# Threshold attention and a squared-ReLU layer: own buffers for the low words' integers, and own step orders for the first two periods

## The chip, the cores and the metric

The kernel runs on one core of a Trainium2 chip. Its engines work side by side and meet through semaphores: PE (TensorE, matrix products and transposes; PEld is its weight load), DVE (VectorE), ACT (ScalarE), POOL (GpSimd) and SP (SyncE, which here only issues DMAs). The metric is the device time of one execution in microseconds (us); the median of three runs is given.

## The reference

Attention over 8 batches, 8 heads, 576 rows and head size 64, in which only scores within `tau` of their row's maximum count; its output, rearranged to 4608 rows of 512, goes through two matrix products with a squared ReLU between them. `q`, `k`, `v` are float32; `w_in` and `w_out` come as float64.

```python
scores = scale * np.matmul(q, k.transpose(0, 1, 3, 2))
thresh = np.max(scores, axis=-1, keepdims=True) - tau
scores = np.where(scores >= thresh, scores, -1000000000.0)
scores = scores - np.max(scores, axis=-1, keepdims=True)
attn = np.exp(scores)
attn = attn / (np.sum(attn, axis=-1, keepdims=True) + 1e-09)
attn_out = np.matmul(attn, v).astype(np.float32)
...
x = np.ascontiguousarray(attn_out.transpose(0, 2, 1, 3)).reshape(B * S, H * D)
h = np.maximum(x @ w_in, 0.0)
return (h * h @ w_out).astype(np.float32)
```

## The kernel before, in words

The kernel has three stages: attention (up to about 510 us of the profile), the first matrix product (`hidden_layer`, line 825) and the second (`output_layer`, line 960). The two products are done by a scheme with fewer multiplications, which needs sums and differences of blocks of the operands; much of POOL's and DVE's work is that. The change touches the attention stage only.

**Units and periods.** The 64 heads are taken as 32 pairs (two heads side by side in 128 partitions). A pair's 576 rows make four units of 128 rows; the last 64 rows of two pairs share a fifth unit. A period (`period(p)`, line 608) starts two units, A = 2p and B = 2p + 1, and finishes the two before. Within a period the order on every engine is the order in which a list of step names is gone through; there are two lists, `PLAIN` (line 592) and `CONVERTING` (line 597), the second for periods in which a weight chunk is converted (p = 2 to 34). Each engine executes its own instructions strictly in that order. The steps that matter here:

- `SA`, `SB` (`scores`, line 423; PE at L434): the scores of A and B, into a PSUM tile `sc` of six banks. A0 means unit A, first head; B1 unit B, second head.
- `topA0` ... `topB1` (L452, DVE): the row minimum of the negated scores, with a copy of the scores to SBUF.
- `powA0` ... `powB1` (L462, ACT): the exponentials. `leastA`, `leastB` (L459, POOL): the threshold.
- `maskA0` ... `maskB1` (L467, DVE): the exponentials are set to zero below the threshold, and summed. It has two inputs in SBUF.
- `over`, `inv` (L474 POOL, L477 DVE): the reciprocal of the sums.
- `U`, `V`, `W` (`fill`; PE at L380 and L515) with `eU`, `eV`, `eW` (`filled`; ACT at L523): the weights are transposed through PSUM; `U` and `V` use the one buffer of the pool `pt`, `W` the middle banks of `sc`.
- `PV` (L532, PE): weights times `v`. `x`, `xm` (L642, L654): its eviction, its scaling, and the store of x to DRAM (L578).
- `T` (`turn_some` and `turn`, PE at L398) with `eT` (ACT at L403 and L411): q or k of a later pair is transposed, into what `spots()` gives (banks 1 and 4 of `sc`, which also hold scores), and evicted. q of pair 1 is turned in period 0, k of pair 1 in period 1, q of pair 2 in period 2. When `eT` is gone through, it also asks for the loads of a later pair (`ask_ahead`, line 343): after pair 0 that is pair 1, after pair 1 both pairs 2 and 3.
- `fetch` (line 178; SP at L191): the load of a weight chunk, 128 x 1024 words of 32 bits, for the period after the next.
- `c1` to `c6` (`convert1` to `convert6`): a float64 chunk becomes float32 with integer operations on its low and high words, which lie alternately in the buffer `raw`. `c1` (L205, ACT) takes the high words' absolute value, `c2` (L212, POOL) scales the low words to integers in place, `c3` (L219, POOL) clamps, `c4` and `c5` (L227, L235, DVE) shift and merge, `c6` (L245, POOL) adds the two. A chunk's `c1`, `c2` and `c3` stand in one period, `c4` to `c6` in the next: chunk 0 begins in period 2, chunk 1 in period 3.

**Queues.** Nearly all DMAs are issued by SP, in the order of the steps; each takes SP some 0.4 to 0.6 us. There are eight semaphores for them in turn, so a DMA is issued only when the eighth before it has landed. Loading q of a pair takes two DMAs (L294), loading k seven (L308 four times, L315 twice, L316 once). A load of v is one (L326).

**Banks.** Each PSUM access is declared by `touch` (line 355): two accesses to the same bank by different engines wait for each other, others do not. So a `top` that reads bank 1 waits for a turn that was written to bank 1 ahead of it in the list.

**Start.** Lines 1014 to 1031: loads of pair 0, some transposes of the identity that write nothing of use (`keep_busy`), the turns of pair 0, then the periods from p = -2; after period 0 come 20 more such transposes.

The arena is one SBUF tile that is cut up by hand (`Region`, line 19); `cv` is the region of the conversion's buffers.

Of the kernel before, what the change touches and what calls it, by code (L numbers as in the profile page):

```python
# [10 lines left out]
FP32 = mybir.dt.float32  # L11
# [37 lines left out]
def kernel(  # L49
# [49 lines left out]
    ARENA = 27264  # L99
    X_SIZE = 7 * BANK + 3 * 7 * P  # L100
    X_AT = (ARENA - X_SIZE, ARENA - 2 * X_SIZE)
    arena = ctx.enter_context(tc.tile_pool(name="arena", bufs=1)).tile([P, ARENA], FP32, name="arena")
    sb, cv = Region(arena, 0, X_AT[0]), Region(arena, X_AT[0], ARENA)

    ident = const.tile([P, P], FP32, name="ident")
    make_identity(nc, ident)
# [101 lines left out]

    def convert2(m):
        if m in parts:  # L210
            lo = parts[m][0]
            nc.gpsimd.tensor_scalar(out=lo, in0=lo.bitcast(U32), scalar1=2.0**-29, scalar2=None, op0=ALU.mult)  # L212

    def convert3(m):
        if m not in parts:
# [175 lines left out]
    def turn(i, which, spots, other=None):  # L391

        nat, to = loaded.pop((i, which)), places(i)
        of = [nat[:, t, :] for t in range(FULL)] + ([loaded.pop((i, 2))] if which else [])
        for t, x in enumerate(of):
            for r, (spot, at) in enumerate(spots):
                rows = ds(r * HALF, HALF)
                made = nc.tensor.transpose(spot[:, ts(t, HALF)], x[rows, :], ident[rows, rows])  # L398
                touch("turns", made, at, BANK)
        half = FULL * HALF  # L400

        def scaled(to, spot):
            touch("turned", nc.scalar.activation(out=to, in_=spot[0], func=AF.Identity, scale=qscale[:, :]), spot[1], BANK, i)  # L403

        def then():
            part = lambda r, x, n: (spots[r][0][:, ds(x, n)], spots[r][1])
            if which:
                for r, n in ((0, half), (1, half + REST)):
                    spot = part(r, 0, n)
                    copy_by = other if r and other else nc.scalar.copy  # L410
                    touch("turned", copy_by(to[1][:, ds(r * half, n)], spot[0]), spot[1], BANK, i)  # L411
                scaled(to[2], part(0, half, REST))
                ask_ahead(i, 1)
            else:
                for r in range(2):
                    scaled(to[0][:, ds(r * half, half)], part(r, 0, half))
                ask_ahead(i, 0)

        return then
# [179 lines left out]
        powA1 powB0 c4 eT inv x maskA1 maskA0 W leastB maskB0 c5 eV c2 powB1 c6 eW maskB1 xm  # L599
    """.split()  # L600

    def spots():
        return [(sc[:, ds(b * BANK + REST, (FULL + 1) * HALF)], b * BANK) for b in (1, 4)]

# [3 lines left out]
    def period(p):  # L608

        A, B_, a, b = 2 * p, 2 * p + 1, 2 * p - 2, 2 * p - 1  # L610
        m, turns = p - 2, TURNS.get(p, ())
        late, pt = {"W": []}, {}

        def fills(f, m):
            if has(2 * m):
                pt[f] = pt_pool.tile([P, 2, BANK], FP32, tag="pt", name="pt")
                fill(m, f, pt[f])

        def evict(f, m):
            if has(2 * m):  # L620
                filled(m, f, pt[f], 2 * BANK if f == "W" else None)

        def W():
            if has(2 * m + 2):
                pt["W"] = middle()
                fill(m + 1, "W", pt["W"], 2 * BANK)

        def turn_some():
            late["turn"] = [turn(g // 2, g % 2, spots()) for g in turns]

        def PV():
            if has(2 * m):
                values(m)

        def values_out():
            if not has(2 * m):
                return
            late["x"] = x = sb.tile([P, 2, P], FP32, tag="x", bufs=2, name="x")
            for j in range(2):
                from_ = sc[:, ds(5 * j * BANK, P)]  # L640
                if converts(p):
                    made = nc.scalar.copy(x[:, j, :], from_)  # L642
                else:
                    made = nc.vector.tensor_tensor(  # L644
                        out=x[:, j, :], in0=from_, in1=wT[m][:, ts(SCALE_AT + j, P)], op=ALU.mult
                    )
                touch("x", made, 5 * j * BANK, P, m)

        def given_out():
            if has(2 * m):  # L650
                x = late.pop("x")
                if converts(p):
                    both = x[:, :, :].rearrange("p j n -> p (j n)")
                    nc.gpsimd.tensor_tensor(out=both, in0=both, in1=wT[m][:, ds(SCALE_AT * P, 2 * P)], op=ALU.mult)  # L654
                wT.pop(m)
                valued(m)
                give_x(m, x)
            ask(False)

        def scored_a():  # L660
            if has(A):
                scores(A, False)
                scores(A, True)
                scores(B_, True)
                softmax(A)

        def scored_b():
            if has(A):
                scores(B_, False)
                softmax(B_)  # L670

        def every(key):
            for then in late.get(key, ()):
                then()

        steps = {
            "U": lambda: fills("U", m), "V": lambda: fills("V", m + 1), "W": W, "T": turn_some,
            "eU": lambda: evict("U", m), "eV": lambda: evict("V", m + 1), "eW": lambda: evict("W", m + 1),
            "eT": lambda: every("turn"),
            "SA": scored_a, "SB": scored_b,  # L680
            "PV": PV, "x": values_out, "xm": given_out,
            "c1": lambda: convert1(begun(p)), "c2": lambda: convert2(begun(p)),
            "c3": lambda: convert3(begun(p)), "c4": lambda: convert4(begun(p - 1)),
            "c5": lambda: convert5(begun(p - 1)), "c6": lambda: convert6(begun(p - 1)),
            "s1": lambda: sums_due(p) and sums_step(), "s2": lambda: sums_due(p) and p < 60 and sums_step(), "fetch": lambda: fetch(begun(p + 2)),
        }
        steps["over"] = lambda: do(a, "over")
        steps["inv"] = lambda: do(a, "inverse")
        for letter, n in (("A", A), ("B", B_)):
            for what, name in (("least", "least"),):  # L690
                steps[what + letter] = lambda n=n, name=name: do(n, name)
            for what, name in (("top", "top"), ("pow", "power"), ("mask", "mask")):
                for j in range(2):
                    steps[f"{what}{letter}{j}"] = lambda n=n, name=name, j=j: do(n, name, j)
        for name in CONVERTING if converts(p) else PLAIN:
            steps[name]()
        for n in (A, B_):
            if has(n) and units[n][1] == FULL:
                for i in units[n][0]:
                    turned.pop(i)  # L700
# [301 lines left out]
    with tc.manual_schedule():  # L1002
        with ExitStack() as stack:
            sc = stack.enter_context(tc.tile_pool(name="sc", bufs=1, space=PSUM)).tile([P, 6 * BANK], FP32, name="sc")
            pt_pool = stack.enter_context(tc.tile_pool(name="pt", bufs=1, space=PSUM))

            def keep_busy(times, to=None):

                if to is None:
                    to = pt_pool.tile([P, 2, BANK], FP32, tag="pt", name="idle")[:, 0, 0:P]  # L1010
                for _ in range(times):
                    nc.tensor.transpose(to, ident[:, :], ident[:, :])

            load_q(0)
            load_k(0)
            read_tau()
            first = sb.tile([P, 4, 4], FP32, tag="small", bufs=4, name="small")
            nc.scalar.activation(out=first[:, 0, :], in_=ident[:, 0:4], func=AF.Exp)
            load_v(0)
            keep_busy(15)  # L1020
            pq = pt_pool.tile([P, 2, BANK], FP32, tag="pt", name="pq")
            turn(0, 0, [(pq[:, r, :], None) for r in range(2)])()
            keep_busy(8, sc[:, ds(5 * BANK, P)])
            turn(0, 1, spots(), nc.vector.tensor_copy)()
            for i in range(1, 3):
                load_v(i)
            for p in range(-2, NU // 2 + 3):
                period(p)
                if p == 0:
                    keep_busy(20)  # L1030
                if X_FIRST <= p < X_FIRST + 4:
                    load_x(0, XPARTS[p - X_FIRST :][:1])
                if p == X_FIRST + 4:
                    summing.append(prepare_x(0, lambda op, out, x, y: op(nc.gpsimd, out, x, y)))
            for _ in range(60):
                sums_step()
            ask()
# [186 lines left out]
```

## Time and profile before

| | us |
|---|---|
| median of 3 runs | 1307.08 (1306.43 to 1308.34) |
| the profiled execution's own time | 1308.12 |
| its span, first to last instruction | 1306.3 |
| attention stage | 0 to about 510 |
| first product (PE L825) | about 512 to 880 |
| second product (PE L960) | about 924 to 1306 |

The page's first part gives each engine's busy share of the span: PE 98%, DVE 77%, ACT 65%, POOL 70%. These are averages over three stages with different limits. The second part shows DVE at nine tenths or more in 14 of the first 15 of 40 slices of 32.7 us, that is in most of the attention stage, and PE at nine tenths from its second slice on. The groups of the conversion on POOL are L212 (32 times, 2035 ns each), L245 (32 times, 1479 or 1478 ns) and L219 (32 times, 613 ns). Start and length of single instructions are read from the timeline, whose rows are: start, length, engine, line, operation, what it writes and reads, how many were merged, and in brackets the idle time before it with what ended that.

### The profile page before, as it was taken

What the parts mean: (1) busy time and instruction counts of PE and PEld (TensorE: products, weight loads), DVE (VectorE), ACT (ScalarE), POOL (GpSimd) and SP (SyncE); (2) the same over time, 40 slices, a digit from 0 to 9 for tenths busy, and PEclk for the clock granted to TensorE, in tenths of its full rate; (3) what the DMA queues carried; (4) which work ended last, traced back from release to release, by engine and by line L of the source; (5) the groups of instructions that cost most, each with busy time, mean ns of one, the idle gap of its engine ahead of it and who ended that gap; (6) DMA issues with size and microseconds to landing.
All of it is one profiled execution on the core that took longest, in us unless ns stands there. A gap on an engine that the chain in (4) does not pass through costs nothing.

```text
span 1306.3 us, 47872 instructions
## 1 busy us (share of the span) xinstructions
PE 1284.5 (98%) x19483; PEld 1159.8 (89%) x19483; DVE 1010.8 (77%) x2431; ACT 845.7 (65%) x1498; POOL 916.4 (70%) x1023
## 2 busy tenths in 40 slices
PE   8999999999999999999999999999999999999998
PEld 5777777677777777999999999999999999999998
DVE  5999999999999996877787778777646654665463
ACT  5999999888898985657665766675523432433240
POOL 2777778755555320978897789768777777777775
PEclk9999999999999999999999999999999999999999
DMA  6565666544333313466556665569645234522511
GB/s 153 145 160 140 169 182 188 147 103 104 89 78 79 79 41 80 133 200 218 182 181 194 203 208 164 180 247 393 245 158 162 63 105 158 162 68 96 162 34 33
DMA packets 247035, 192.12 MB, mean 147 GB/s; under 512 B 97184, under 2 KB 195488, under 8 KB 246816
## 3 DMA queue, kind: packets, MB, share of 16 engines
q1 hardware_dynamic: 245504, 188.66, 48.5%
q8 instruction: 153, 2.51, 0.8%
q14 instruction: 66, 0.54, 0.2%
q10 hardware_dynamic: 1312, 0.41, 0.1%
HBM read 116.65 MB, written 72.35 MB: 145 GB/s over the span
## 4 chain that ended last, share of the span: by engine, by line
PE 87%; ACT 5%; DMA 3%; DVE 3%; issue 1%; POOL 1%; SPq 0%; ACTq 0%; DVEq 0%; POOLq 0%
PE po L960 29%; PE ph L825 28%; PE sc L532 11%; PE sc L434 10%; PE pt L380 5%; DVE arena L452 3%; ACT arena L462 2%; PE sc L515 2%; DMA wall<-w 2%; PE sc L398 2%; ACT arena L523 1%; PE sc L380 1%; DMA g<-arena 1%; ACT arena L403 0%; ACT c L771 0%
## 5 line engine op out<-in xcount | busy, mean ns | idle before, releaser
L125 POOL TENSOR_TENSOR arena<-arena 128x512 f32<-128x512 f32 (+1 forms) x314 | 378.1, 1223 | 129.1 <-DVE arena L125 115.1
L960 PE MATMUL po<-wall,arena 128*128 128x128 f32 x3528 | 394.7, 275 | 1.4 <-ACT arena L737 1.4
L960 PEld LDWEIGHTS po<-wall,arena 128*128 128x128 f32 x3528 | 394.3, 192 | 1.8 <-ACT arena L737 1.8
L825 PE MATMUL ph<-arena,wall 128*128 128x128 f32 x3528 | 394.2, 275 | 0.7 <-DVE arena L644 0.7
L825 PEld LDWEIGHTS ph<-arena,wall 128*128 128x128 f32 x3528 | 394.0, 192 | 0.8 <-issue 0.8
L125 DVE TENSOR_TENSOR arena<-ph,arena 128x512 f32<-128x512 f32 x378 | 256.3, 688 | 86.3 <-PE ph L825 63.2
L122 POOL TENSOR_TENSOR arena<-arena 128x128 f32<-128x128 f32 (+2 forms) x314 | 255.4, 814 | 53.8 <-DMA arena<-w 37.6
L125 DVE TENSOR_TENSOR arena<-po,arena 128x128 f32<-128x128 f32 x378 | 108.4, 290 | 168.6 <-PE po L960 164.5
L467 DVE SCALAR_TENSOR_TENSOR arena<-arena 128x576 f32<-128x576 f32 x288 | 237.4, 860 | 1.3 <-POOL arena L459 0.8
L452 DVE TENSOR_SCALAR_CACHE_REDUCE arena<-sc 128x576 f32<-128x576 f32 x288 | 205.0, 747 | 14.6 <-ACT arena L523 4.8
L462 ACT ACTIVATE arena<-arena 128x576 f32<-128x576 f32 x288 | 208.1, 773 | 11.8 <-DVE arena L452 8.5
L771 ACT COPY c<-arena 128x512 f32<-128x512 f32 (+1 forms) x303 | 173.5, 579 | 49.6 <-DVE arena L122 41.7
L532 PEld LDWEIGHTS sc<-arena 64*64 64x64 f32 x5760 | 159.2, 133 | 36.7 <-DVE arena L452 20.2
L532 PE MATMUL sc<-arena 64*64 64x128 f32 (+1 forms) x5760 | 180.8, 262 | 2.7 <-DVE arena L452 1.3
L434 PE MATMUL sc<-arena 64*64 64x64 f32 (+1 forms) x2304 | 176.9, 414 | 6.2 <-ACT arena L403 4.2
L122 DVE TENSOR_TENSOR arena<-arena,c 128x512 f32<-128x512 f32 (+1 forms) x267 | 174.9, 663 | 5.5 <-ACT c L771 4.0
L523 ACT COPY arena<-pt 128x1024 f32<-128x1024 f32 x144 | 146.4, 1017 | 30.5 <-PE pt L380 29.4
L737 ACT COPY arena<-po 128x128 f32<-128x128 f32 x63 | 16.6, 264 | 186.7 <-PE po L960 184.0
L380 PEld LDWEIGHTS pt<-ident,arena 64*128 64x128 f32 x2304 | 83.4, 139 | 39.4 <-ACT arena L523 30.1
L737 ACT COPY arena<-ph 128x512 f32<-128x512 f32 x63 | 36.6, 581 | 123.1 <-PE ph L825 122.5
L434 PEld LDWEIGHTS sc<-arena 64*64 64x64 f32 x2304 | 74.3, 134 | 45.1 <-ACT arena L403 15.1
L380 PE MATMUL pt<-ident,arena 64*128 64x64 f32 x2304 | 102.2, 228 | 2.3 <-ACT arena L523 2.3
(50 smaller groups left out, 922.2 us busy)
## 6 DMA issues: line engine op xcount, KB each, us to landing
g<-arena SPq DMA_DIRECT2D x144, 256.0 KB, 2.6
arena<-g SPq DMA_DIRECT2D x144, 256.0 KB, 4.6
w<-arena SPq DMA_DIRECT2D x60, 256.0 KB, 2.4
wall<-w SPq DMA_DIRECT2D x49, 256.0 KB, 5.2
arena<-w SPq DMA_DIRECT2D x44, 256.0 KB, 3.3
arena<-in_v_dram SPq DMA_DIRECT2D x32, 288.0 KB, 4.0
out_dram<-arena SPq DMA_DIRECT2D x70, 128.0 KB, 2.2
arena<-in_q_dram SPq DMA_DIRECT2D x64, 128.0 KB, 4.0
```

The source lines that it names most:

```text
L122: e.tensor_tensor(out=out, in0=x, in1=y, op=ALU.subtract)
L125: e.tensor_tensor(out=out, in0=x, in1=y, op=ALU.add)
L380: made = nc.tensor.transpose(pt[:, r, ts(slot, HALF)], of[rows, :], ident[rows, rows])
L434: made = nc.tensor.matmul(sc[at, ds(to, count)], lhs, kT[rows, ds(at_k, count)], start=True, stop=True)
L452: made = nc.vector.tensor_scalar(out=s[:, j, :], in0=sc[:, ds(at, S)], scalar1=1.0, scalar2=None, op0=ALU.mult, op1=ALU.min, accum_out=nmx ...
L462: nc.scalar.activation(out=w[:, :, j, :], in_=of(j), func=AF.Exp, bias=nmx[:, j : j + 1], scale=-1.0)
L467: nc.vector.scalar_tensor_tensor(out=w[:, :, j, :], in0=of(j), scalar=thr[:, j : j + 1], in1=w[:, :, j, :], op0=ALU.is_le, op1=ALU.mult, a ...
L523: touch("weights", nc.scalar.copy(joined(to), whole(pt, 0, count)), at, 2 * BANK, m)
L532: made = nc.tensor.matmul(sc[ds(u * D, D), ds(5 * j * BANK + row, count)], loaded_v[i][rows, (c - (u != j)) % CH, :], wT[m][rows, ds(weigh ...
L771: nc.scalar.copy(c, y)
L825: nc.tensor.matmul(to[:, j, :], W_IN[m, k][:, ts(j, P)], of[k][:, m - 1, :], start=(not more and j == 0), stop=True, skip_group_check=True,)
L960: nc.tensor.matmul(to, g[:, j, :], w[:, j, :], start=(not more and j == 0), stop=(j == 3), skip_group_check=True)
```

## The change

Four things are edited.

1. The arena gets 512 more columns, and `convert2` writes the low words' integers to one of two buffers of 512 words, in a row, in place of every second word of `raw`. `convert6` reads them there.
2. Periods 0 and 1 have lists of steps of their own (`BEGIN_WITH`). In the list of period 1, `eT` stands ahead of `fetch`.
3. In these two periods `T` writes to a buffer of the pool `pt` and not to `spots()`.
4. The loads of q and k of pair 1 are asked for ahead of the first load of v, and the 20 transposes after period 0 are gone.

```diff
--- before.py
+++ after.py
@@ -99,8 +99,9 @@
     ARENA = 27264
     X_SIZE = 7 * BANK + 3 * 7 * P
     X_AT = (ARENA - X_SIZE, ARENA - 2 * X_SIZE)
-    arena = ctx.enter_context(tc.tile_pool(name="arena", bufs=1)).tile([P, ARENA], FP32, name="arena")
-    sb, cv = Region(arena, 0, X_AT[0]), Region(arena, X_AT[0], ARENA)
+    arena = ctx.enter_context(tc.tile_pool(name="arena", bufs=1)).tile([P, ARENA + BANK], FP32, name="arena")
+    sb, cv = Region(arena, 0, X_AT[0]), Region(arena, X_AT[0], ARENA - BANK)
+    cv.ring("low", [ARENA, ARENA - BANK])
 
     ident = const.tile([P, P], FP32, name="ident")
     make_identity(nc, ident)
@@ -208,8 +209,10 @@
 
     def convert2(m):
         if m in parts:
-            lo = parts[m][0]
-            nc.gpsimd.tensor_scalar(out=lo, in0=lo.bitcast(U32), scalar1=2.0**-29, scalar2=None, op0=ALU.mult)
+            lo, hi, a = parts[m]
+            low = cv.tile([P, WC], I32, tag="low", bufs=2, name="low")
+            nc.gpsimd.tensor_scalar(out=low, in0=lo.bitcast(U32), scalar1=2.0**-29, scalar2=None, op0=ALU.mult)
+            parts[m] = (low, hi, a)
 
     def convert3(m):
         if m not in parts:
@@ -599,6 +602,17 @@
         powA1 powB0 c4 eT inv x maskA1 maskA0 W leastB maskB0 c5 eV c2 powB1 c6 eW maskB1 xm
     """.split()
 
+    BEGIN_WITH = {
+        0: """
+            SA SB fetch topA0 T topA1 leastA topB0 topB1 leastB powA0 powA1 eT powB0 powB1
+            maskA0 maskA1 maskB0 maskB1
+        """.split(),
+        1: """
+            SA SB T eT fetch over topA0 topA1 leastA inv V topB0 topB1 leastB powA0 powA1 eV W
+            powB0 eW maskA0 maskA1 powB1 maskB0 maskB1
+        """.split(),
+    }
+
     def spots():
         return [(sc[:, ds(b * BANK + REST, (FULL + 1) * HALF)], b * BANK) for b in (1, 4)]
 
@@ -626,7 +640,11 @@
                 fill(m + 1, "W", pt["W"], 2 * BANK)
 
         def turn_some():
-            late["turn"] = [turn(g // 2, g % 2, spots()) for g in turns]
+            free = None
+            if turns and p < 2:
+                pq = pt_pool.tile([P, 2, BANK], FP32, tag="pt", name="pq")
+                free = [(pq[:, r, :], None) for r in range(2)]
+            late["turn"] = [turn(g // 2, g % 2, free or spots()) for g in turns]
 
         def PV():
             if has(2 * m):
@@ -692,7 +710,7 @@
             for what, name in (("top", "top"), ("pow", "power"), ("mask", "mask")):
                 for j in range(2):
                     steps[f"{what}{letter}{j}"] = lambda n=n, name=name, j=j: do(n, name, j)
-        for name in CONVERTING if converts(p) else PLAIN:
+        for name in BEGIN_WITH.get(p) or (CONVERTING if converts(p) else PLAIN):
             steps[name]()
         for n in (A, B_):
             if has(n) and units[n][1] == FULL:
@@ -1016,6 +1034,8 @@
             read_tau()
             first = sb.tile([P, 4, 4], FP32, tag="small", bufs=4, name="small")
             nc.scalar.activation(out=first[:, 0, :], in_=ident[:, 0:4], func=AF.Exp)
+            ask_ahead(0, 0)
+            ask_ahead(0, 1)
             load_v(0)
             keep_busy(15)
             pq = pt_pool.tile([P, 2, BANK], FP32, tag="pt", name="pq")
@@ -1026,8 +1046,6 @@
                 load_v(i)
             for p in range(-2, NU // 2 + 3):
                 period(p)
-                if p == 0:
-                    keep_busy(20)
                 if X_FIRST <= p < X_FIRST + 4:
                     load_x(0, XPARTS[p - X_FIRST :][:1])
                 if p == X_FIRST + 4:
```

## The prediction

> **What bounds the kernel now.** I read the page's parts 1 and 2, then the busy time by windows, then the timeline engine by engine, because the shares of part 1 mix three stages. The change lies in the attention stage, and there first in a steady stretch:
>
> ```profile
> 40.00:230.00 190.00, 187.06 (x4634) 140.69 (x4634) 189.50 (x511) 183.61 (x331) 152.36 (x189) 1.00 0.62 164
> ...
> 163.57 0.78 DVE L467 SCALAR_TENSOR_TENSOR arena<-arena 128x576 f32<-128x576 f32 x1
> 163.79 2.04 POOL L212 TENSOR_SCALAR arena<-arena 128x512 int32<-128x512 uint32 x1
> 164.28 1.22 DVE L467 SCALAR_TENSOR_TENSOR arena<-arena 128x576 f32<-128x576 f32 x1
> 165.43 0.81 DVE L467 SCALAR_TENSOR_TENSOR arena<-arena 128x576 f32<-128x576 f32 x1
> ...
> 167.00 1.48 POOL L245 TENSOR_TENSOR arena<-arena 128x512 int32<-128x512 int32 x1 [1.17 <-DVE arena L235]
> ```
>
> The window's columns are its length, then busy PE, PEld, DVE, ACT, POOL, then the granted clock, DMA share and GB/s. DVE is idle for 0.5 us in 190: it alone sets the period of a converting stretch, 7.08 us from one first `top` to the next. ACT has 190 - 183.61 = 6.4 us of air, 0.24 a period. POOL, where part 1 of the change lies, idles 1.17 us ahead of L245, waiting for DVE. The second mask takes 1.22 us instead of 0.81 when L212 runs.
>
> Then the start, the only place where DVE is not full:
>
> ```profile
> 10.57 0.76 DVE L452 TENSOR_SCALAR_CACHE_REDUCE arena<-sc 128x576 f32<-128x576 f32 x1 [3.08 <-PE sc L398]
> 16.63 0.76 DVE L452 TENSOR_SCALAR_CACHE_REDUCE arena<-sc 128x576 f32<-128x576 f32 x1
> 18.11 2.78 ACT L462 ACTIVATE arena<-arena 128x576 f32<-128x576 f32 x4 [2.55 <-DVE arena L452]
> 20.80 0.67 ACT L411 COPY arena<-sc 128x256 f32<-128x256 f32 x2
> 21.74 2.04 PE L434 MATMUL sc<-arena 64*64 64x512 f32 x24 [1.47 <-ACT arena L403]
> 25.37 0.76 DVE L452 TENSOR_SCALAR_CACHE_REDUCE arena<-sc 128x576 f32<-128x576 f32 x1 [2.80 <-issue]
> ```
>
> Periods 0, 1, 2 begin their tops at 10.57, 16.63, 25.37. The first waits for a turn of pair 1 (L398) that shares bank 1. Ahead of the third DVE idles 2.80 us: the evictions of k of pair 1 (L411 at 20.80) stand behind four exponentials, and the scores of period 2 wait for them (21.74).
>
> **Part 1, own buffers: nothing.** L212 reads every second word and writes every second word. It begins while the first mask runs, which ends at 164.28; from there it needs 165.83 - 164.28 = 1.55 us. L219, equal in size and in a row, takes 0.61. So the new L212 lies between 0.49 + 0.61 = 1.10 us and the 2.04 of today; I take 1.10, as only the steps of the operands and the integer types differ. What this saves (0 to 0.94 us) goes to POOL's idle time ahead of L245, which still waits for DVE's L235. The second mask loses 0.41 us, about the time of 512 reads; the reads stay as they are, so I leave the 0.41 in all 33 periods. L245 is 1.48 now and 1.28 as an f32 sum in rows of the same size (L122): 0 to 0.2 us each, hidden likewise, but for the last one (259.3, the next mask waits behind it): 0.2 at most in the sum.
>
> The page "SBUF — State Buffer" of the Trainium skill (section "Who interferes with whom") says the port pair shared by VectorE and GpSimd is an exclusive lock for a whole instruction, and that a VectorE instruction with two SBUF inputs contends with a GpSimd instruction that reads SBUF. By the whole-instruction lock the second mask could not have ended at 165.50, ahead of L212's end at 165.83; the trace agrees only that the two get into each other's way.
>
> **Parts 2 to 4, the start.** Pitches from the rows: top 0.68 (10.57, 11.26, 11.94), mask 0.74, exponential 0.70 (2.78 / 4). Period 0: its scores end at 8.96 (L434, 7.64 + 1.32), and `topA0` no longer waits for the turn, so tops run from 9.07 to 11.8. ACT makes two exponentials, the q eviction (0.82) and two more, 9.85 + 4 x 0.70 + 0.82 = 13.5. Masks from 11.8, the last behind the last exponential, end at 14.8 (now 16.5). Period 1: tops 14.8 to 17.6; k is evicted ahead of the exponentials, before 14.9. ACT then has four exponentials, `eV` (1.01) and `eW` (0.61), from 15.6 with waits for the tops to 19.9; the last mask ends at 20.7 (now 22.6). Period 2: PE has `W` done at 18.5, then SA (1.32), U (0.71), T (0.46): tops could begin at 21.0, or at 22.2 if the clock halves (2.04, 1.12, 0.64, the rows at 21.74 to 24.62). That is 3.2 to 4.4 us ahead of 25.37. The dropped 20 transposes free PE from 11.41 to 13.81, off this path. The first v is issued 5.6 us later and needed only by PV of period 2.
>
> **Where it goes.** The new list of period 1 has `eT` ahead of `fetch`; `eT` asks for k of pairs 2 and 3, so the load of weight chunk 1 is moved behind 14 DMAs on SP's queue:
>
> ```profile
> 13.51 0.43 SPq L191 DMA_DIRECT2D arena<-in_moe_w_in_dram  x1
> 14.06 2.33 SPq L294 DMA_DIRECT2D arena<-in_q_dram  x4
> 16.43 2.63 SPq L191 DMA_DIRECT2D arena<-in_moe_w_in_dram  x1
> 19.11 1.26 SPq L308 DMA_DIRECT2D arena<-in_k_dram  x2
> ...
> 28.77 0.59 SPq L191 DMA_DIRECT2D arena<-in_moe_w_in_dram  x1
> ...
> 32.65 0.68 ACT L205 ACTIVATE arena<-arena 128x512 f32<-128x512 f32 x1
> ```
>
> Today chunk 1 is issued at 16.43, its ACT step `c1` comes at 32.65. The 14 k DMAs take from 19.11 to 28.77. In the new order the first k DMA stands where chunk 1 stood. Chunk 1's issue was held 2.63 us there, with chunk 0 and four q DMAs still under way (landings 19.23 to 21.29) and nothing else in sight, so I let k be held too, to 19.2: the k issues end 0.5 us earlier, and chunk 1 is issued at about 28.3. L191's landings are 4.1 / 4.6 / 6.6 us (min, median, max): it lands at L = 32.9. Were k not held, its fourth DMA would still wait for the eighth before it, chunk 0, at 19.23: 11 more of 0.65 and one fetch stall of 0.4 as in the 1.02 us L315 at 25.10 put chunk 1 at 26.9 and L at 31.0 or later. The late end is 28.8 + 6.6 = 35.4.
>
> Behind `c1` of period 3 ACT's queue holds all of the period's exponentials, which were ready at 29 to 30: DVE waits with the masks, PE with the next scores. From `c1` to the end of the period's last exponential ACT needs 38.33 - 32.65 = 5.68, without its 0.1 of waiting 5.6; one mask pitch (0.74) follows. So period 4's tops begin at L + 6.34; now at 39.66. Gain = 33.32 - L: 0.4 at L = 32.9, 2.3 at 31.0, a loss of 2.1 at 35.4. DVE is full from there to 250 us, and all later stages follow one another, so the shift reaches the end unchanged.
>
> Sum: 1308.12 - 0.4 = 1307.7 on the profiled execution, which is 1.04 above the median; against the median 1307.08 - 0.4 = **1306.7**.
>
> **Rivals.**
> A. Chunk 1 doesn't bind, and the start's whole 3.2 to 4.4 us remain. It would have to land by 29; its earliest place in the queue says 31. 1303.3. Chance 0.10.
> B. k isn't held: L about 31.4, gain 1.9, 1305.2. For it: a k DMA is small; against: the 2.63. Chance 0.14.
> C. The second mask's delay follows L212's length, as the skill's lock rule would have it. Up to 0.41 x 33 periods, but ACT's air caps it at 0.24 x 33 = 8; I take 6 and 1301. Against: the delay ended while L212 still ran. Chance 0.07.
> D. Slower: PE, idle while ACT waits, gets half a clock.
>
> ```profile
> 18.76:22.17 3.41, 1.43 (x24) 0.87 (x28) 3.38 (x10) 3.41 (x8) 0.80 (x1) 1.00 0.81 209
> 22.18:25.59 3.41, 3.41 (x52) 2.40 (x48) 0.61 (x3) 1.62 (x3) 0.00 (x0) 0.50 0.41 91
> ```
>
> After 3.41 us with PE busy for 1.43 of them, the next 3.41 us ran at 0.50. In the new kernel PE finishes PV and W of period 3 at about 33 to 34 and then waits for ACT's evictions at L + 3.7 = 36.6. At half a clock SA, U and T of period 4 take 0.72 + 0.41 + 0.18 = 1.3 more, of which 0.65 is left over after slack. It decides from L = 33.3 on; with L = 34.9 (28.3 + 6.6) it gives 1.6 + 0.65 = 2.2 slower, 1309.3. Chance 0.17. "TensorE: Matmul & The Clock Gate" of the Trainium skill (Part 1, on the clock gate) gives half rate after an idle window of about 3.4 us; the trace agrees on the 3.41, but its window was 42% busy, not idle.
> E. L212 stays at 2.04 us because the conversion of types costs it, and the buffers do nothing: the same 1306.7, part of my forecast.
>
> **How the numbers follow.** My forecast has 0.52: L from 32.4 to 33.7, 1306.2 to 1307.5. About 0.2% (2.6 us) is what a measurement of this kernel can tell from no change. Faster by more: A and C, and a little of B, 0.18. Slower by more: half of D, 0.10. Within: 0.72. The range takes B, the nearer part of A and most of D: 1303.5 to 1309.2.
>
> **What would show it.** The first tops at about 9.1, 14.8 and 21 to 22; chunk 1 (L192 there, SP) issued near 28.3; ACT idle for some 3 us ahead of the second `c1`, released by that DMA; then masks of period 3 at 35, period 4's tops near 39.3. L214 near 1.1 us, the mask beside it still 1.2, 7.08 us a period. I am wrong if period 4's tops begin before 37 or after 41, or if the masks beside L214 go below 1.1.

## The result, and the profile after

The changed kernel takes 1312.62 us (median of 5 runs, 1312.30 to 1316.32) and the kernel before 1307.08 us (1306.43 to 1308.99); the ratio is 1.0047, with a 95% interval of 1.0034 to 1.0060. It is slower, by more than the 0.2% that the prediction set as its bound, and above the predicted range. Two of its five runs (1315.60 and 1316.32 us) had a lower granted clock, 0.995 and 0.996 against 0.997, and no trace of them was kept. The profiled execution took 1312.31 us with a span of 1310.5 us, 4.2 us above the span of before.

The 4.2 us are the sum of a gain and a loss of two different parts of the change. Measured at the first tops of the periods: period 4's tops begin at 37.83 us, not at 39.66 (1.83 us gained). The 30 periods from there to period 34 take 219.78 us, not 213.47 (6.31 us lost). From period 34 to the end, 0.27 us come back. -1.83 + 6.31 - 0.27 = 4.21.

Loss first. The window of the steady stretch, and the groups of the conversion on POOL, of the changed kernel (a group's row ends with busy time, mean length in ns, and idle time ahead of it):

```profile
40.00:230.00 190.00, 183.43 (x4481) 136.06 (x4477) 186.85 (x493) 180.17 (x321) 172.57 (x182) 1.00 0.60 162
```

```profile
L462 POOL TENSOR_SCALAR arena<-arena,tau_p 128x2 f32<-128x2 f32 x144 | 79.8, 554 | 43.6 <-DVE arena L455 38.4 <-DVE arena L480 1.8
L214 POOL TENSOR_SCALAR arena<-arena 128x512 int32<-128x512 uint32 x32 | 65.0, 2032 | 2.5
...
L248 POOL TENSOR_TENSOR wall<-arena 128x512 int32<-128x512 int32 x16 | 28.7, 1795 | 7.7 <-DVE arena L238 7.7
L248 POOL TENSOR_TENSOR arena<-arena 128x512 int32<-128x512 int32 x16 | 28.7, 1794 | 9.4 <-DVE arena L238 6.1 <-DMA xT<-arena 2.9 <-DMA arena<-in_moe_w_out_dram 0.4
```

DVE, full before (189.50 of 190), now idles 3.15 us there, and POOL is busy 20 us more. The integer scaling of the low words (L214, before L212) still takes 2.03 us: writing in a row saved nothing. The sum (L248, before L245) went from 1.48 to 1.80 us. The timeline of one period of the changed kernel (start, length, engine, line, operation, what it writes and reads) shows how POOL's 0.32 us reaches DVE:

```profile
169.12 1.80 POOL L248 TENSOR_TENSOR arena<-arena 128x512 int32<-128x512 int32 x1 [0.44 <-DVE arena L238]
170.88 0.73 POOL L672 TENSOR_TENSOR arena<-arena 128x256 f32<-128x256 f32 x1
171.58 0.61 POOL L222 TENSOR_SCALAR arena<-arena 128x512 f32<-128x512 f32 x1
172.17 0.29 POOL L462 TENSOR_SCALAR arena<-arena,tau_p 128x2 f32<-128x2 f32 x1
172.39 0.42 DVE L230 TENSOR_SCALAR arena<-arena 128x512 int32<-128x512 int32 x1
172.52 0.37 POOL L477 TENSOR_SCALAR arena<-arena 128x4 f32<-128x4 f32 x1
172.93 0.18 DVE L480 RECIPROCAL arena<-arena 128x4 f32<-128x4 f32 x1
172.99 0.90 POOL L462 TENSOR_SCALAR arena<-arena,tau_p 128x2 f32<-128x2 f32 x1
173.03 0.79 DVE L470 SCALAR_TENSOR_TENSOR arena<-arena 128x576 f32<-128x576 f32 x1
173.74 0.81 DVE L470 SCALAR_TENSOR_TENSOR arena<-arena 128x576 f32<-128x576 f32 x1
173.97 2.04 POOL L214 TENSOR_SCALAR arena<-arena 128x512 int32<-128x512 uint32 x1
174.48 1.25 DVE L470 SCALAR_TENSOR_TENSOR arena<-arena 128x576 f32<-128x576 f32 x1
```

Behind the sum POOL has, in order, x's scaling (L672), the clamp of the next chunk (L222), a threshold (L462), and the clamp of the four sums (L477) that DVE's reciprocal (L480) reads; the masks stand behind the reciprocal. The same steps before:

```profile
163.01 0.23 POOL L474 TENSOR_SCALAR arena<-arena 128x4 f32<-128x4 f32 x1
163.14 0.42 DVE L227 TENSOR_SCALAR arena<-arena 128x512 int32<-128x512 int32 x1
163.34 0.38 POOL L459 TENSOR_SCALAR arena<-arena,tau_p 128x2 f32<-128x2 f32 x1
163.48 0.17 DVE L477 RECIPROCAL arena<-arena 128x4 f32<-128x4 f32 x1
```

Before, POOL's clamp of the four sums ended at 163.24, 0.24 us ahead of the reciprocal. Now it falls beside DVE's L230, takes 0.37 us, and ends at 172.89; the reciprocal follows at 172.93, though DVE was through with L230 at 172.81. Taken as medians over 18 periods from the period's first top, the reciprocal begins at 3.25 us and not at 3.05, and the one mask that is delayed beside the scaling takes 1.26 us and not 1.21. 0.20 + 0.05 = 0.25 is nearly the whole growth of the period, from 7.07 to 7.33 us. Thirty times 0.25 is 7.5; two periods of before happened to be longer (7.64 and 7.81, in each a wait of DVE of 0.5 us), hence some 6.3 in this pair of traces.

Now the gain. Tops of periods 0 to 2 and the wait for chunk 1, of the changed kernel:

```profile
10.07 0.76 DVE L455 TENSOR_SCALAR_CACHE_REDUCE arena<-sc 128x576 f32<-128x576 f32 x1 [1.59 <-PE sc L437]
...
15.75 0.75 DVE L455 TENSOR_SCALAR_CACHE_REDUCE arena<-sc 128x576 f32<-128x576 f32 x1
...
23.41 0.76 DVE L455 TENSOR_SCALAR_CACHE_REDUCE arena<-sc 128x576 f32<-128x576 f32 x1 [1.46 <-PE sc L401]
...
16.33 2.74 SPq L311 DMA_DIRECT2D arena<-in_k_dram  x2
...
27.51 1.06 SPq L192 DMA_DIRECT2D arena<-in_moe_w_in_dram  x2
...
31.58 0.69 ACT L206 ACTIVATE arena<-arena 128x512 f32<-128x512 f32 x1 [0.30 <-DMA arena<-in_moe_w_in_dram]
```

The tops come 0.5, 0.9 and 2.0 us earlier. The k load is held where chunk 1's was (of the 2.74 us, the first issue takes 2.08), chunk 1 is issued at 27.51 and landed at 31.55; `c1` waits for it 0.30 us. TensorE ran at half rate from 17.69 to 24.51 us, 6.83 us in place of the 3.41 of before. How the start comes out differs from one execution to the next; the runs below show by how much.

### The profile page after: what moved, and what is told of

The parts are those of the page before. It is cut to its first block, busy times and chain, and to the rows that moved or that the text cites. A ratio compares the mean times of both kernels' runs of the same rounds, so it can differ in the third digit from the quotient of the medians.

```text
span 1310.5 us, 47836 instructions
## 1 busy us (share of the span) xinstructions
PE 1286.1 (98%) x19463; PEld 1159.3 (88%) x19463; DVE 1014.1 (77%) x2431; ACT 848.0 (65%) x1498; POOL 944.6 (72%) x1023
## 4 chain that ended last, share of the span: by engine, by line
PE 78%; ACT 3%; DVE 2%; DMA 1%; issue 1%; POOL 0%; ACTq 0%; POOLq 0%; SPq 0%
PE ph L843 30%; PE po L978 29%; PE sc L535 7%; PE sc L437 6%; PE pt L383 4%; DVE arena L455 2%; ACT arena L465 1%; ACT arena L526 1%; PE sc L401 1%; PE sc L518 1%; DMA wall<-w 1%; PE sc L383 0%; DMA g<-arena 0%; ACT arena L406 0%; DMA w<-arena 0%
## 5 line engine op out<-in xcount | busy, mean ns | idle before, releaser
L462 POOL TENSOR_SCALAR arena<-arena,tau_p 128x2 f32<-128x2 f32 x144 | 79.8, 554 | 43.6 <-DVE arena L455 38.4
```

## The experiments

Line numbers differ by one or two between these kernels; each sentence names the step.

**The orders alone.** Part 1 is taken back.

```diff
-            lo, hi, a = parts[m]
-            low = cv.tile([P, WC], I32, tag="low", bufs=2, name="low")
-            nc.gpsimd.tensor_scalar(out=low, in0=lo.bitcast(U32), scalar1=2.0**-29, ...
-            parts[m] = (low, hi, a)
+            lo = parts[m][0]
+            nc.gpsimd.tensor_scalar(out=lo, in0=lo.bitcast(U32), scalar1=2.0**-29, ...
```

> The change without its first part: the low words' integers stay in place, the lists of periods 0 and 1, the turns in the transposes' banks and the early loads stay. Theory 1 (the loss is the separate buffers': the sum on POOL takes 1.80 us instead of 1.48, POOL's chain from it to the reciprocal no longer fits into DVE's period, 7.33 us a period instead of 7.07): the sum is back at 1.48, the period at 7.07 to 7.08, the gain of the start (1.8 us at period 4's first top: 37.83 against 39.66) reaches the end, about 1305.3. Theory 2 (the new start throws the steady stretch into a slower pattern, in which DVE waits for the reciprocal's input, whatever the buffers are): period 7.3, about 1312.

Measured: 1307.78 us (1304.84 to 1309.87) against 1308.46 for the kernel before in the same comparison, ratio 0.9995 (0.9985 to 1.0006). The sum is 1.48 us again and the period 7.07: the loss is part 1's. But the start's gain did not show in the median, and the profiled execution shows a cause: from period 3's first top to period 4's it took 8.30 us.

```profile
32.03 0.70 ACT L206 ACTIVATE arena<-arena 128x512 f32<-128x512 f32 x1 [1.80 <-DMA arena<-in_moe_w_in_dram]
```

`c1` of period 3 waited 1.80 us for chunk 1 here, six times as long as in the trace of the changed kernel, though the orders are the same.

**The buffers alone.** The kernel before with part 1 only.

```diff
...
-            lo = parts[m][0]
-            nc.gpsimd.tensor_scalar(out=lo, in0=lo.bitcast(U32), scalar1=2.0**-29, ...
+            lo, hi, a = parts[m]
+            low = cv.tile([P, WC], I32, tag="low", bufs=2, name="low")
+            nc.gpsimd.tensor_scalar(out=low, in0=lo.bitcast(U32), scalar1=2.0**-29, ...
+            parts[m] = (low, hi, a)
```

> The kernel before with the separate buffers alone. Theory 1: the sum on POOL at 1.80, the period at 7.33 from the first converting periods on, start as before (tops at 10.6, 16.6, 25.4), about 1307.1 + 1.8 + the 5.5 of the changed kernel = 1314.4. Theory 2: period 7.07, about 1307.

Measured: 1315.15 us (1314.54 to 1315.81) against 1308.46, ratio 1.0055 (1.0037 to 1.0072). Sum 1.80, scaling 2.03, period 7.32 us, the reciprocal 0.20 us late. Part 1 alone costs about what was expected, 6.7 us for 7.3. But its start, which has the orders of before, isn't the expected one: TensorE had no half-rate window in this execution, period 2's tops came at 24.34 us and not at 25.4, and period 4's at 38.55, 1.11 us earlier than in the trace of before.

**A buffer apart, but in steps.** The integers go to the same 1024 words outside `raw`, but to every second word: the two buffers lie in each other's gaps.

```diff
...
-            low = cv.tile([P, WC], I32, tag="low", bufs=2, name="low")
+            low = pick(arena[:, ds(ARENA - BANK, 2 * BANK)].bitcast(I32), m % 2)
```

> The changed kernel with the integers in buffers apart from the raw words, but at every second word (the two buffers lie in each other's gaps). Theory 1a (what makes the sum slow is that one operand is in a row and the other in steps): the sum at 1.48, period 7.07, about 1305.3. Theory 1b (what makes it slow is that its operands no longer lie side by side in one buffer): 1.80, period 7.33, 1312.6.

Measured: 1323.27 us (1320.93 to 1325.29), ratio 1.0115 (1.0093 to 1.0136). The sum grew again, to 2.01 us, and with it the wait:

```profile
165.76 0.44 DVE L229 TENSOR_SCALAR arena<-arena 128x512 int32<-128x512 int32 x1
166.34 0.23 POOL L476 TENSOR_SCALAR arena<-arena 128x4 f32<-128x4 f32 x1
166.60 0.18 DVE L479 RECIPROCAL arena<-arena 128x4 f32<-128x4 f32 x1 [0.40 <-POOL arena L476]
```

Here the trace names the wait: 0.40 us for POOL. The period is 7.59 us. So a row is not what makes the sum dearer; it looks as if the neighbouring place made it cheap. Period 3 to 4 took 12.88 us in this execution, on which more below.

**The thresholds ahead of the clamp.** In `CONVERTING`, `leastA over` stand ahead of `c3`, so that the four sums are clamped 0.6 us earlier.

```diff
-        fetch SA U eU T SB topA0 s1 c1 topA1 topB0 c3 V PV leastA over powA0 topB1
+        fetch SA U eU T SB topA0 s1 c1 topA1 leastA over topB0 c3 V PV powA0 topB1
```

> The changed kernel with POOL's threshold and sum steps (leastA, over) set ahead of the clamp (c3) in the list of converting periods. They are 0.61 us earlier, which is more than DVE waits for the reciprocal's input (about 0.2 us a period). Theory 1 (POOL's chain to the reciprocal is what lengthens the period): the sum stays at 1.80 but the period is back at about 7.07 to 7.12, about 1305.3 to 1307. Theory 2 (DVE loses the time to a port that POOL holds longer, not to a wait): the period stays near 7.3, 1312.

Measured: 1319.30 us (1317.55 to 1321.19), ratio 1.0085 (1.0067 to 1.0103), period 7.46 us. The reciprocal waits no more, and yet the period is longer than the changed kernel's 7.33:

```profile
164.05 0.62 POOL L222 TENSOR_SCALAR arena<-arena 128x512 f32<-128x512 f32 x1
164.19 0.76 DVE L230 TENSOR_SCALAR arena<-arena 128x512 int32<-128x512 int32 x1
164.87 0.16 DVE L480 RECIPROCAL arena<-arena 128x4 f32<-128x4 f32 x1
```

POOL's clamp of the chunk now falls beside DVE's shift (`c4`, L230), which takes 0.76 us and not 0.42. The wait was removed, and contention of 0.34 us took its place; the expectation missed that. (The time holds a late start too; see the table further down.)

**The clamp last.** The other way out: `c3` behind `c2`.

```diff
-        fetch SA U eU T SB topA0 s1 c1 topA1 topB0 c3 V PV leastA over powA0 topB1
-        powA1 powB0 c4 eT inv x maskA1 maskA0 W leastB maskB0 c5 eV c2 powB1 c6 eW maskB1 xm
+        fetch SA U eU T SB topA0 s1 c1 topA1 topB0 V PV leastA over powA0 topB1
+        powA1 powB0 c4 eT inv x maskA1 maskA0 W leastB maskB0 c5 eV c2 c3 powB1 c6 eW maskB1 xm
```

> The changed kernel with the clamp c3 (L222, 0.62 us on POOL) moved in the list of CONVERTING from ahead of the thresholds to behind c2 (L214): POOL's chain sum, xm, threshold, clamp of four values, threshold is 0.62 us shorter, and VectorE's c4 no longer meets POOL's c3. The sum stays at 1.80 us. Nothing is left out. Theory 1 (the steady loss is POOL's chain behind the longer sum, which ends 0.26 us too late for the reciprocal): the reciprocal no longer waits, and the period is 7.05 to 7.15 us; the time is 1303.5 to 1308 as chunk 1's landing has it. Rival (POOL is simply too full, 6.8 us of a period of 7.07: whatever leaves one place delays another): the sum now begins 0.2 us or more later behind L214 and L222, the next chain is late again, and the period stays at 7.25 us or more, the time 1311 or more.

Measured: 1319.31 us (1317.68 to 1322.56), ratio 1.0084 (1.0062 to 1.0106), period 7.48 us. The first half of the expectation held: the reciprocal begins at 3.05 us of its period, as before the change. But again:

```profile
172.68 0.87 POOL L222 TENSOR_SCALAR arena<-arena 128x512 f32<-128x512 f32 x1
...
173.00 1.12 DVE L238 SCALAR_TENSOR_TENSOR arena<-arena 128x512 int32<-128x512 int32 x1
```

The clamp now meets DVE's merge (`c5`, L238), which takes 1.12 us and not 0.68. The rival put the time right and the way wrong: POOL isn't too full (it idles 0.65 us ahead of the sum, waiting for `c5`), but what it does at the new place isn't free. A top (0.75 us in every one of these kernels, beside the sum, x's scaling or the clamp) reads PSUM; `c4`, `c5` and the masks read SBUF alone, and in these kernels the first of them that begins beside the scaling or the clamp loses 0.34 to 0.46 us. (The next one need not: in the changed kernel `c5` begins 0.34 us before the scaling ends, and takes 0.69 us.) "SBUF — State Buffer" of the Trainium skill (section "Who interferes with whom") says so: DVE contends with POOL where an instruction has two inputs in SBUF or runs in a two-port mode, and not with at most one input there; for the tops, `c5` and the masks these rows agree. `c4` has one input in SBUF, and no row shows whether it runs in such a mode.

**Both addends in rows.** The bit operation of `c5` writes to `a`, so that both addends lie in rows of their own.

```diff
-            out=hi, in0=hi, scalar=-(1 << 30), in1=a, op0=ALU.bitwise_and, op1=ALU.bitwise_or
+            out=a, in0=hi, scalar=-(1 << 30), in1=a, op0=ALU.bitwise_and, op1=ALU.bitwise_or
...
-        nc.gpsimd.tensor_tensor(out=a, in0=hi, in1=lo, op=ALU.add)
+        nc.gpsimd.tensor_tensor(out=a, in0=made, in1=lo, op=ALU.add)
```

> The changed kernel, with the bit operation (L242) writing its result into the buffer `a`, which is in a row, instead of back into every second word of the loaded chunk: now both addends of the sum (L249) lie in rows, each in a buffer of its own. Nothing is left out. Theory 1c (the sum is dear where its two addends are laid out differently or far apart: 1.48 as neighbours in one pair, 1.80 with one of them in a row elsewhere, 2.01 with one of them in steps elsewhere): steps cost 0.2 us for each addend that has them, so the sum should fall to 1.5 to 1.65 us, the reciprocal's wait for POOL should go, and the period should be 7.07 to 7.15 us, the time 1306 to 1308. Theory 1d (an integer sum costs less only where both addends are neighbours in one pair): the sum stays at 1.75 to 1.85 us and the period at 7.3 us, the time at 1312 to 1315. A third outcome, a sum of about 1.28 us (POOL's row for a float sum in rows), would say that steps are the whole price.

Measured: 1312.84 us (1311.88 to 1317.47), ratio 1.0045 (1.0028 to 1.0063). The sum stays at 1.78 us and the period at 7.32: rows don't help. This left two readings: the place of the addends in itself, or who gets in POOL's way.

**The sums by themselves.** Eight POOL operations on 128x512 words behind the last step, four times over, twice with DVE idle and twice beside a stream of DVE sums of two SBUF inputs. (The comments are not in the kernel.)

```diff
...
+        add(put(0), high, low)      # neighbours in one pair
+        add(put(1), high, near)     # in steps, 256 bytes apart
+        add(put(2), high, apart)    # in steps, far apart
+        add(put(3), high, row)      # one in steps, one in a row
+        add(put(4), row2, row)      # two rows
+        nc.gpsimd.tensor_tensor(out=f(put(5)), in0=f(row2), in1=f(row), op=ALU.add)
+        scaled(put(6), low)
...
```

> The kernel with the orders alone and chunk 1 asked for first, and behind its last step, where TensorE needs the weights no more, eight POOL operations on 128x512 words of the weight buffer, four times over: twice with VectorE idle, twice beside a stream of VectorE sums. They change nothing that is put out; the time of this run isn't read, only the lengths of these operations. Theory 1e (the length of an integer sum is a matter of where its addends lie): with VectorE idle too, the sum of two words that are neighbours in a pair takes about 1.48 us, with one of them 256 bytes or many kilobytes away 1.75 to 2.0 us, in two rows 1.8 us, the float sum in two rows 1.28 us, and the scaling of integers 2.0 us in steps and in a row. Theory 1f (the sum's length in the changed kernel is contention: VectorE's masks hold what POOL reads): with VectorE idle all integer sums take one length, 1.5 us or less, and they spread only beside the stream.

The run's own time holds the added operations and isn't compared. The run's kernel is that of chunk 1 first, the next experiment. The timeline of POOL with DVE idle (the second time over; at the first, DVE's last instructions were still running), the five integer sums in the order of the listing, then the scaling:

```profile
1306.22 1.04 POOL L1210 TENSOR_TENSOR wall<-wall 128x512 int32<-128x512 int32 x1
1307.22 1.49 POOL L1210 TENSOR_TENSOR wall<-wall 128x512 int32<-128x512 int32 x1
1308.66 1.49 POOL L1210 TENSOR_TENSOR wall<-wall 128x512 int32<-128x512 int32 x1
1310.11 1.29 POOL L1210 TENSOR_TENSOR wall<-wall 128x512 int32<-128x512 int32 x1
1311.36 1.26 POOL L1210 TENSOR_TENSOR wall<-wall 128x512 int32<-128x512 int32 x1
1313.92 1.51 POOL L1211 TENSOR_SCALAR wall<-wall 128x512 int32<-128x512 uint32 x1
```

| 128x512 words | DVE idle | beside the stream (2 values) | in the kernels |
|---|---|---|---|
| integer sum, neighbours | 1.04 | 1.54, 1.21 | 1.48 (before) |
| integer sum, both in steps apart | 1.49 | 1.93, 1.94 | 2.01 (apart, in steps) |
| integer sum, one in steps, one in a row | 1.29 | 1.74, 1.73 | 1.80 (after) |
| integer sum, two rows | 1.26 | 1.71, 1.70 | 1.78 (both in rows) |
| float sum, two rows | 1.26 | 1.70, 1.70 | |
| scaling, from steps | 1.51 | 1.83, 1.85 | 2.03 (after) |
| scaling, from a row | 1.49 | 1.66, 1.66 | |

The four sums keep their order in all three columns, so the place of the addends is what makes the sum longer: 1.29 - 1.04 = 0.25 us with DVE idle, 0.32 in the kernels. Why neighbours are cheap was not tried. The expected sizes, taken from the kernels, were too large for an idle DVE: in the kernels each sum takes 0.44 to 0.52 us more. That this is contention with DVE is inferred; it fits the stream, and one sum of the changed form that begins ahead of the mask beside it (thresholds first, at 39.41 us): that sum takes 1.30 us, and the mask 1.72 in place of 0.81. An integer sum of two rows costs what a float sum does, and the scaling costs 1.5 us from a row as well.

**Chunk 1 first.** The orders alone, with `fetch` ahead of `eT` in the list of period 1.

```diff
...
-            SA SB T eT fetch over topA0 topA1 leastA inv V topB0 topB1 leastB powA0 powA1 eV W
+            SA SB T fetch eT over topA0 topA1 leastA inv V topB0 topB1 leastB powA0 powA1 eV W
```

> The run of the orders alone (part 1 undone) with one word moved in the first list of period 1: the fetch of chunk 1 stands ahead of the transposes' evictions, so that chunk 1 is asked for ahead of the 14 k and q loads and not behind them. Theory 2 (the start's gain is cut by chunk 1's landing: ScalarE waited 0.30, 1.80, 3.60 and 4.93 us for it in four traces where it landed at 31.55, 32.01, 34.19 and 34.41 us): chunk 1 is issued near 16 us and lands before 25 us; ScalarE doesn't wait for it; periods 2 to 4 begin near 22.8, 30.0 and 37.0 us; the period from 3 to 4 is 7.0 to 7.3 us and no half-rate window of TensorE falls behind 30 us; the span is 2 to 3 us under that of the kernel before, the time 1304 to 1306. Rival 2b (the loads behind chunk 1 come 0.6 to 2 us later and take its place): the scores of period 2 wait for k, its tops begin at 23.5 to 25 us, and the time is 1306 to 1308, no better than the run of the orders alone.

Measured: 1303.46 us (median of 11 runs, 1301.72 to 1306.08) against 1307.74, ratio 0.9971 (0.9960 to 0.9982): faster than both kernels.

```profile
16.18 2.31 SPq L192 DMA_DIRECT2D arena<-in_moe_w_in_dram  x1
...
28.99 0.68 ACT L206 ACTIVATE arena<-arena 128x512 f32<-128x512 f32 x1
...
35.79 0.75 DVE L453 TENSOR_SCALAR_CACHE_REDUCE arena<-sc 128x576 f32<-128x576 f32 x1
```

Chunk 1 is issued at 16.18, `c1` waits for nothing, and period 4's tops begin at 35.79, 3.87 us ahead of before and 1.2 ahead of the expectation. The k loads behind it came late for nothing. But these 3.87 us are not the order's alone, for TensorE was faster at the start of this execution than in that of the changed kernel: eight transposes of the identity (PE, from 5.3 and 5.5 us) took 1.09 us here and 1.97 there, the first tops began at 8.99 and 10.07, and the half rate that came later lasted 3.41 us and 6.83. The run of the sums by themselves has the same orders as this one, but 1.86 us for the transposes, first tops at 9.95 and 6.83 us at half rate:

```profile
30.93 0.69 ACT L206 ACTIVATE arena<-arena 128x512 f32<-128x512 f32 x1
...
37.64 0.75 DVE L453 TENSOR_SCALAR_CACHE_REDUCE arena<-sc 128x576 f32<-128x576 f32 x1
```

There too `c1` waits for nothing, and period 4's tops begin only 0.19 us ahead of the changed kernel's 37.83. So in the trace of the changed kernel the place of `fetch` cost some 0.2 to 0.3 us, and the rest of what parts it from 35.79 goes with TensorE's rate. The times are the firmer ground: 4.3 us under the kernel before over 11 runs, where the orders alone, in a comparison of their own, came out 0.7 us under it over 10. The place of one `fetch` is thus worth some 3 us in the median.

What it gave away varied from execution to execution. Six traces with `eT` ahead of `fetch`, where L is the landing of chunk 1 and L + 6.34 the prediction's formula for period 4's tops:

| run | first k issue held | chunk 1 issued | L | `c1` waits | L + 6.34 | tops of period 4 |
|---|---|---|---|---|---|---|
| both in rows | 1.39 | 27.04 | 31.15 | 0.35 | 37.49 | 37.37 |
| after | 2.08 | 27.51 | 31.55 | 0.30 | 37.89 | 37.83 |
| orders alone | 2.30 | 27.67 | 32.01 | 1.80 | 38.35 | 38.27 |
| clamp last | 2.95 | 28.62 | 32.76 | 1.71 | 39.10 | 40.09 |
| thresholds first | 3.33 | 29.14 | 34.19 | 3.60 | 40.53 | 41.94 |
| apart, in steps | 3.39 | 30.12 | 34.41 | 4.93 | 40.75 | 42.10 |

The formula holds within 0.12 us for the first three. With a wait of 0.3 us that tests little, as the start's own pace gave 37.64 above; the orders alone, with 1.80, are the test. The run with the clamp last begins 1.0 us later than the formula says, with no half-rate window there: the last mask of period 3 and the sum begin together (38.20 and 38.24), and the mask takes 1.96 us in place of 0.81. The last two begin 1.4 us later. (These late starts are in the times of the three kernels as well; for the steady stretch their periods say more.) The windows of the run apart, in steps, and its first top of period 4 show what takes it there (PEclk is the last column but two):

```profile
31.62:35.03 3.41, 1.55 (x50) 1.23 (x42) 0.73 (x3) 0.60 (x2) 0.00 (x0) 1.00 0.92 297
35.04:41.86 6.82, 4.48 (x64) 3.27 (x64) 4.18 (x10) 5.29 (x13) 6.00 (x6) 0.50 0.68 182
...
42.10 0.76 DVE L454 TENSOR_SCALAR_CACHE_REDUCE arena<-sc 128x576 f32<-128x576 f32 x1 [1.45 <-PE sc L400]
```

While ACT waits for chunk 1, PE is busy for 1.55 of 3.41 us, and the next 6.82 us run at half rate; the top then waits 1.45 us for PE: rival D of the prediction, as it was described. The run with the thresholds first has such a stretch too, from 37.25 to 44.08 us, but there PE accounts for 0.61 us, and 0.91 goes to the mask of 1.72 us named above.

**Chunk 1 first, and PE kept busy.** The same, with the 20 transposes behind period 0 put back.

```diff
...
                 period(p)
+                if p == 0:
+                    keep_busy(20)
```

> The kernel of the run before, and the 20 filling matmuls after period 0 are back, which the change took out. Theory 2c (TensorE's rate is halved from 16.3 to 23.1 us because it stood idle for much of the stretch before, and the fillers prevent it): the half-rate window goes or shrinks to 3.4 us, the tops of period 2 begin 0.5 to 1 us earlier (21.8 to 22.3 us instead of 22.8), and the time is 0.5 to 1 us under that of the run before, 1303.5 to 1305. Rival 2d (the fillers only stand ahead of period 1's matmuls): tops of period 1 come 0.3 to 1 us later, the half-rate window stays, and the time is 0.3 to 1 us over that of the run before.

Measured: 1306.45 us (1304.45 to 1308.15), ratio 0.9987 (0.9978 to 0.9996), 3 us worse than without them. Both theories were half right.

```profile
15.00:18.40 3.40, 2.36 (x48) 1.13 (x42) 2.56 (x8) 1.20 (x4) 0.48 (x2) 1.00 0.99 281
18.41:21.80 3.39, 3.31 (x88) 2.44 (x88) 2.54 (x7) 3.39 (x6) 0.29 (x1) 1.00 0.93 239
```

The half rate is gone altogether (it was in the run of the buffers alone too, so one trace doesn't show that the fillers did it). But period 1's tops begin at 15.84 us, not at 14.67, and period 3's at 29.47, not at 28.73. From period 0's first top to period 1's it takes 6.72 us, and 5.68 in each of the eight traces of the new start without the fillers: 1.04 us is their price there. That trace also has one period of 7.64 us; where the rest of the 3 us comes from stays open.

## Why the prediction was wrong

- **The step that failed** is part 1's last term: "L245 is 1.48 now and 1.28 as an f32 sum in rows of the same size (L122): 0 to 0.2 us each, hidden likewise". The sum got 0.32 us longer, not up to 0.2 shorter, and "hidden" became 0.25 us in each period, 6.3 us from period 4 to 34; by itself this part makes the kernel 6.7 us slower. 1.48 was the price of two neighbouring words, and moving one of them was a change to the sum, which the prediction bounded only downward. The float sum in rows looked like a floor but is dearer than the neighbours: 1.26 against 1.04 us by themselves. The two rows compared were not alike: 1.28 is about what such a sum takes with DVE idle, while 1.48 is 0.44 us more than the neighbours take then.
- **The cover was misread.** POOL's 1.17 us of idle time lie ahead of the sum and hide what comes ahead of it, L212. What lies behind the sum was covered by 0.24 us only, the space between POOL's clamp of the four sums and DVE's reciprocal. "Hidden likewise" named the wrong cover. A sum 0.32 us longer, and a clamp 0.14 us longer where it slid beside L230, use that up and leave some 0.20 us a period; the mask adds 0.05.
- **The scaling.** 1.10 was taken from 1.10 to 2.04; it stayed at 2.03. Rival E had the length. By itself it takes 1.49 us from a row and 1.51 in steps, so it isn't the steps; that it is the conversion of types, as E says, no run takes apart. This cost the forecast nothing.
- **The mask's delay.** Left at 0.41, measured at 0.45, in the third mask and not in the second; rival C had its condition not met, since L214's length didn't change.
- **The start.** Tops were forecast at 9.1, 14.8 and 21 to 22.2, and came at 10.07, 15.75 and 23.41 in the trace of after, at 8.99, 14.67 and 21.55 with chunk 1 first; PE ran 6.83 us at half rate in the first and 3.41 in the second. The 5.7 us from period 0 to 1 were right (5.68), but the 20 transposes were not off the path: with them it is 6.72. k was held as forecast, chunk 1 was issued at 27.51 (28.3 forecast) and landed after 4.0 us (4.6 forecast): L = 31.55, not 32.9. The formula 33.32 - L gives 1.77, measured 1.83. Chunk 1 binds, as forecast, but in this trace by 0.30 us only: the same start without that wait, and with as much half rate (sums by themselves), gained 2.02. So the close agreement is in part luck: what was missing to the 3.2 to 4.4 us of the whole start went mostly with TensorE's rate here, and not with chunk 1. L's spread was wider in the traces (31.2 to 34.4) than the central case allowed. (The 6.6 us of its late end were misread: they are those of the issue at 16.43 and hold its 2.63 us in the queue; the longest other landing took 5.7.)
- **Rival D** forecast a slower kernel by the wrong road for this trace, but the mechanism exists. Where it stands alone (apart, in steps) its price was 1.35 us beyond the formula; 0.65 was taken after slack.
- **Rival A**, the whole start at 3.2 to 4.4 us if chunk 1 doesn't bind, needed one `fetch` moved and a fast TensorE at the start: 3.87 us in one trace of that order, 2.02 in the other.

## What to carry to other kernels

When operands move, cost the instruction that reads them anew, in both directions; a row that costs less for a similar shape is no floor. Idle time ahead of an instruction covers what comes before it and says nothing of what follows: for that, find the next thing that another engine waits for, and measure its slack. Before moving POOL's work out of a wait, look at what DVE does at the new place: wide SBUF work beside DVE's SBUF work came back as 0.34 and 0.44 us on DVE in the two tries. And one trace doesn't tell what a start is worth: the same orders began period 4 at 35.79 and at 37.64 us.

## What the runs showed of the hardware

- A POOL sum of two neighbouring words takes 1.04 us for 128x512, with the addends not side by side 1.26 to 1.49 us, float or integer alike (float measured for two rows only).
- Scaling uint32 to int32 on POOL takes 1.49 us from a row and 1.51 in steps, where the float clamp of the same size takes 0.61.
- Beside DVE's stream, a POOL sum of 1.04 to 1.49 us takes 0.44 to 0.50 longer (once 0.17), and a DVE sum of 0.69 takes 1.41 to 1.87. By "SBUF — State Buffer" of the Trainium skill (section "Who interferes with whom") the one that comes first locks the shared ports for a whole instruction; the sums of the stream agree with it, while in the kernel the delayed mask ends before the scaling does (175.73 against 176.01).
- TensorE's clock was halved behind stretches of 3.41 us in which PE was busy for 1.23, 1.55 and 1.74 us, and was not behind one of 3.40 with 2.36. Busy time alone doesn't decide it: the clock was halved behind one with 2.14 (12.85 to 16.26 us, orders alone), and not behind ones with 1.72 (34.44 to 37.85 us, clamp last) and 1.82 (19.71 to 23.12 us, buffers alone).
- TensorE's rate at the start differs between executions of the same orders (chunk 1 first, sums by themselves): eight transposes took 1.09 and 1.86 us, the half rate later on 3.41 and 6.83 us, and period 4 began at 35.79 and 37.64 us.
